# Attention and two gated layers on one core: the fp16 copy of P made by GpSimd, and attention steps dealt to slices by a table

## The chip, the cores and the metric

One core of a Trainium2 chip runs the whole program. The time is device microseconds of one execution; of several executions the median is given. TensorE (PE in the profile, its weight loads PEld) multiplies, VectorE (DVE) and ScalarE (ACT) work element by element, GpSimd (POOL) does selects, clearings and reductions across partitions, and SyncE (SP) issues nearly all DMAs, one after the other in its own order.

## The reference

Inputs are q, k, v of shape (4, 8, 576, 64), a memory `M_prev` and `z_prev` for each head, a gate `beta`, and the weights of two gated feed-forward layers. The reference computes:

```python
scores = where(causal, -1e9, scale * q @ k.T)     # 4 batches, 8 heads, 576 tokens
a      = softmax(scores);  local = a @ v
q_p    = phi(q);           mem   = (q_p @ M_prev) / (q_p @ z_prev + 1e-6)
x      = sigmoid(beta) * mem + (1 - sigmoid(beta)) * local       # 2304 tokens of 512
xn     = x / sqrt(mean(x*x) + 1e-6) * rms_g
x      = (silu(xn @ w_gate) * (xn @ w_val)) @ w_out               # d_ff 1536
out    = (sigmoid(x @ w_gate2) * (x @ w_val2)) @ w_out2
```

All inputs are fp32, and the kernel keeps nearly fp32 accuracy by splitting each operand of a product in a high and a low part (fp32r or fp16) and adding three products. The exponentials P of attention are such an operand.

## The kernel before, in words

The tokens are worked on in five groups. Group -1 holds the first 128 tokens of all four batches (512 tokens), groups 0 to 3 the other 448 tokens of one batch each. A group goes through both gated layers (l = 0 and 1), each cut into 12 slices of 128 hidden columns (f = 0 to 11), so 24 slices in a group. For each slice TensorE makes the gate and value products (`hidden`, 12 matmuls each, line 961), ScalarE and VectorE form the gated value and split it in two (`gated`, lines 981 to 1006), and TensorE adds the slice's share to the output (`out_share`, 12 matmuls, line 1027), one slice behind. The weights come from DRAM through SyncE's queue; in group -1 they are unpacked from 64-bit words, in group 0 they are turned into fp16 pairs (`halve`, lines 830 to 841: sums by ScalarE, an all-reduce by GpSimd at line 832, two scaled passes by ScalarE, two by VectorE) and written back, later they are loaded as pairs (line 903). In group 1 the output weights get the same treatment (`share_steps`, lines 752 to 778).

While the 24 slices of group g run, the attention of group g + 1 is made beside them. It is a list of steps (`att_steps`, 41 of them, 36 for the last), head by head: `v` loads V, `qk` loads and splits keys and queries (tiles kd and qd, one buffer each, lines 210 to 230), `sc` makes scores and the weights P, `av` multiplies P with V, `mem` adds the memory's part for two heads, `meas` measures q and k of the group after it, `vmax`, `vsplit`, `norm`, four `xT` and `units` do what their names say. The scores of a head are laid key by query, 1472 useful columns in a tile `sc`; ScalarE copies them from PSUM (line 550), GpSimd masks four blocks (line 555), VectorE takes the maximum over the key tiles (569, 572), GpSimd over the partitions (574), VectorE subtracts it (575, 580). Then `softmax_weights` (line 234) works in place: ScalarE makes the exponential (237), GpSimd clears the unused first columns of the two halves of P (241 or 244), ScalarE casts the exponential to fp16, the high half (246), and VectorE subtracts that from it, the low half (247). `att_av` uses both as weights (lines 589 to 591). For odd heads of groups 1 to 3 the halves lie in two spare tiles named top, otherwise in a tile pt.

The main loop decides after which slice a step is traced. `done` counts the output shares traced so far in the group (1 to 24). Before the change the share of the list was a straight line between two numbers of the group, kept in `HOLD` and `DUE`:

```python
total = 2 * NF - DUE[g + 1]
wait = HOLD[g + 1]
while used < len(steps) and used < len(steps) * (done - wait) // (total - wait):
    with behind(lagged(AFTER[g + 1])):
        steps[used]()
```

A step's instructions are put behind those of an earlier slice on ScalarE and VectorE (`lagged`), and the loads of a slice's weights behind those of another (`BACK`). Within these bounds the framework lays out each engine's order when the program is built, from the order in which instructions were traced and a model of their durations; on the chip each engine then keeps its order.

Of the kernel before, what the change touches and what calls it, by code (L numbers as in the profile page):

```python
# [10 lines left out]
F32R = mybir.dt.float32r  # L11
# [5 lines left out]
ALU = mybir.AluOpType  # L17
# [9 lines left out]
SW = 1536  # L27
# [8 lines left out]
NSHARE = (2, 1)  # L36

ONE = (1, 12)
DUE = (3, 6, 6, 5, 8)
HOLD = (1, 2, 1, 1, 1)  # L40
BACK = (3, 3)
AFTER = (3, 1, 3, 3)

# [25 lines left out]
def attn_moe_moe_kernel(ctx, tc, qT, kT, qk0, v, mz, beta, w8, rms_g, outT):  # L69
# [6 lines left out]
    nc = tc.nc  # L76
    B, H, D, S = qT.shape
# [3 lines left out]
    NF = w8.shape[1]  # L81
# [3 lines left out]
    const = ctx.enter_context(tc.tile_pool(name="const", bufs=1))  # L85
# [15 lines left out]
        out=tri, in_=tri, compare_op=ALU.is_ge, fill=NEG, base=0, pattern=[[1, 128]], channel_multiplier=-1  # L101
# [25 lines left out]

    q2_ring = []
    for i in range(2):
        t = const.tile([128, S], F32R, name=f"q2_{i}")  # L130
        nc.vector.memset(t[64:128].bitcast(F32), 0.0)
        q2_ring.append(t)
    vh1 = const.tile([128, 5, H, 65], F16, name="vh1")
# [71 lines left out]
    def att_qk(g, u):  # L205
        kd = ap_.tile([128, S], F32, tag="kd", bufs=1, name="kd")
        qd = ap_.tile([128, S], F32, tag="qd", bufs=1, name="qd")[:, 128:S]
        for src, dst, c0 in ((kT, kd, 0), (qT, qd, 128)):
            for j in range(2):
                nc.sync.dma_start(out=dst[64 * j:64 * j + 64], in_=src[g, u, :, c0:S])  # L210
        if g < HALVED:
            q2 = q2_ring[qring[0] % 2]
            qring[0] += 1
            kk = ap_.tile([128, S], F32R, tag="kk", bufs=2, name="kk")
            qq = ap_.tile([128, S], F32R, tag="qq", bufs=2, name="qq")[:, 128:S]
            q2 = q2[:, 128:S]
            nc.scalar.activation(out=kk, in_=kd, func=AF.Copy)
            nc.scalar.activation(out=qq, in_=qd, func=AF.Copy)
            for out, d, hi, r in ((kk, kd, kk, slice(64, 128)), (q2, qd, qq, slice(0, 64))):
                nc.vector.tensor_tensor(out=out[r], in0=d[r], in1=hi[r].bitcast(F32), op=ALU.subtract)  # L220
        else:
            kk = ap_.tile([128, 2, S], F16, tag="kk", bufs=2, name="kk")[:, 0]
            both = ap_.tile([128, 2, S], F16, tag="qq", bufs=2, name="qq")
            qq, q2 = both[:, 0, 128:S], both[:, 1, 128:S]
            nc.gpsimd.memset(q2[64:128], 0.0)
            qs = st["qs", g]
            nc.scalar.activation(out=kk, in_=kd, func=AF.Copy, scale=qs[:, 0:1])
            nc.scalar.activation(out=qq, in_=qd, func=AF.Copy, scale=qs[:, 1:2])
            for out, d, hi, i, r in ((kk, kd, kk, 0, slice(64, 128)), (q2, qd, qq, 1, slice(0, 64))):
                nc.vector.scalar_tensor_tensor(  # L230
                    out=out[r], in0=d[r], scalar=qs[r, i:i + 1], in1=hi[r], op0=ALU.mult, op1=ALU.subtract
                )
        st["qk", g, u] = kk, qq, q2

    def softmax_weights(sc, both, spare):
        sc = sc[:, 64:SW]
        nc.scalar.activation(out=sc, in_=sc, func=AF.Exp, scale=both)  # L237
        if spare:
            pt = [t.bitcast(F16) for t in tops]
            for t in pt:  # L240
                nc.gpsimd.memset(t[:, 0:64], 0.0)
        else:
            pt = ap_.tile([128, 2, SW], F16, tag="pt", name="pt")
            nc.gpsimd.memset(pt[:, :, 0:64], 0.0)
            pt = [pt[:, i] for i in range(2)]
        nc.scalar.copy(out=pt[0][:, 64:SW], in_=sc)
        nc.vector.tensor_tensor(out=pt[1][:, 64:SW], in0=sc, in1=pt[0][:, 64:SW], op=ALU.subtract)
        return pt

# [601 lines left out]
    for i in range(2):  # L851
        t = const.tile([128, SW // 2], I32, name=f"top{i}")
# [502 lines left out]
    def last_of(e):  # L1355
        return next(i for i in reversed(nc.cur_bb.bb.instructions) if i.engine == e)
# [80 lines left out]
    for g in range(-1, B):  # L1437
        n = 512 if g < 0 else S - 128
        steps = list(att_steps(g + 1)) if g + 1 < B else []
# [6 lines left out]
                shares[ONE[1] + f] += share_steps(0, f)  # L1446
            shares[ONE[1] + NF].append(lambda: share_units(0))

        total = 2 * NF - DUE[g + 1]

        wait = HOLD[g + 1]
        if g == 0:
            ring["w"] = NEARLY + NLATE
        done, used = 0, 0
        for l in range(2):
            early = 2 if g < 0 and l == 0 else 0
            ws, hs, halfway = early_ws[:early], early_hs[:early], []
            for f in range(early):
                hidden(ws[f], l, f, 256, g, xt, hs[f], 256, (("mm", "mm"), ("ps", "pa"))[f])
                halfway.append(tuple(last_of(e) for e in (mybir.EngineType.Activation, mybir.EngineType.DVE)))  # L1460
            po = None
            if g == B - 1:
                po = [late[f"po{d // 2}"].tile([128, NMAX], F32, tag=f"po{d}", name="po") for d in range(KD)]
                halves = xt if l == 0 else xh
                xs = token_sums(halves, "c" if l == 0 else "a")
                last_slices(l, n, xt, halves, xs, po)
            for f in range(0 if g == B - 1 else NF + 1):
                if f < NF:
                    if f >= early:
                        if g > 0 and l == 1 and f == NWIDE:  # L1470
                            unit_slices(g)
                        turn = lagged(BACK[g + 1]) if g <= 0 else []
                        if g < 0 and l == 1 and f in (2,):
                            turn = turn + evacuated
                        if g >= 0 and l == 0 and f in (1, 2):
                            turn = turn + tokens_done
                        with behind(turn + (halfway[-1:] if early and f < early + 3 else [])):
                            ws.append(weights(g, l, f))
                        hs.append(htiles(g, l, f))
                        if g == B - 2 and l == 1 and f == NF - 3:  # L1480
                            first_sums(0)
                        hidden(ws[f], l, f, n, g, xh if l == 1 and is_half(g, l, f) else xt, hs[f])
                        marks.append(tuple(last_of(e) for e in (mybir.EngineType.Activation, mybir.EngineType.DVE)))
                if f > 0:
                    if po is None:
                        po = [late[f"po{d // 2}"].tile([128, NMAX], F32, tag=f"po{d}", name="po") for d in range(KD)]
                    out_share(ws[f - 1], hs[f - 1], po, n, f == 1, f == NF)
                    done += 1
                    with ExitStack() as after:

                        if g < 0 and done < 5:
                            traced = nc.cur_bb.bb.instructions
                            for e in (mybir.EngineType.Activation, mybir.EngineType.DVE, mybir.EngineType.SP):
                                after.enter_context(
                                    tc.issue_after(next(i for i in reversed(traced) if i.engine == e))
                                )
                        for step in shares[done]:
                            with behind(lagged(2)):
                                step()
                        while used < len(steps) and used < len(steps) * (done - wait) // (total - wait):  # L1500
                            with behind(lagged(AFTER[g + 1])):
                                steps[used]()
                            used += 1
                            if used == len(steps):
                                tokens_done = [tuple(last_of(e) for e in (mybir.EngineType.Activation, mybir.EngineType.DVE))]
            if g < 0 and l == 0:
                begin.close()
            xn = wide_tokens("cd") if l == 0 else None
            for d in range(KD):
                evacuate(l, d, n, g, po[d], xn)  # L1510
            evacuated = [tuple(last_of(e) for e in (mybir.EngineType.Activation, mybir.EngineType.DVE))]
            if l == 0 and g >= 0:
                xh = half_tokens("b")
                with tc.high_priority(400):
                    halve_tokens(g, n, po, xh)
                    if g >= NSHARE[1]:
                        group_unit()
            if l == 0 and g < 0:
                with tc.issue_after(z["gm"]):
                    token_scale()  # L1520
            xt = xn
# [56 lines left out]
```

## Time and profile before

| what | value |
|---|---|
| median of 3 runs | 1013.51 us (1010.52 to 1014.92) |
| the profiled execution, its own time | 1016.42 us |
| its span, first to last instruction | 1014.6 us |
| mean granted TensorE clock | 0.996 |
| HBM read, written | 187.43 MB, 51.38 MB |

The span is from the first to the last instruction. The page gives the busy time of each engine; a busy TensorE need not be at its peak, since its matmuls overlap in the records. The chain is the work that ended last, followed back from the end to what released each piece. A line with an idle time says how long the engine stood before it and what ended that. DMA issues of SyncE stand on its timeline as SPq.

### The profile page before, as it was taken

What the parts mean: (1) busy time and instruction counts of PE and PEld (TensorE: products, weight loads), DVE (VectorE), ACT (ScalarE), POOL (GpSimd) and SP (SyncE); (2) the same over time, 40 slices, a digit from 0 to 9 for tenths busy, and PEclk for the clock granted to TensorE, in tenths of its full rate; (3) what the DMA queues carried; (4) which work ended last, traced back from release to release, by engine and by line L of the source; (5) the groups of instructions that cost most, each with busy time, mean ns of one, the idle gap of its engine ahead of it and who ended that gap; (6) DMA issues with size and microseconds to landing.
All of it is one profiled execution on the core that took longest, in us unless ns stands there. A gap on an engine that the chain in (4) does not pass through costs nothing.

```text
span 1014.6 us, 19021 instructions
## 1 busy us (share of the span) xinstructions
PE 999.3 (98%) x6721; PEld 700.0 (69%) x6721; DVE 832.1 (82%) x1826; ACT 654.7 (65%) x1238; POOL 201.8 (20%) x339
## 2 busy tenths in 40 slices
PE   9999999999999999999999999999999999999998
PEld 6878887888666676666666765555567556876885
DVE  6989999997769998775998977757779776995883
ACT  7668887786678888674778676535456353543452
POOL 4203221141004233300424432002133100000000
PEclk9999999999999999999999999999999999999999
DMA  9599998986894676498779856995544256836521
GB/s 350 180 373 398 345 352 257 376 308 200 272 368 172 224 251 229 177 322 240 246 257 322 266 179 224 309 340 167 174 144 167 83 159 212 284 135 226 201 84 37
DMA packets 102561, 243.74 MB, mean 240 GB/s; under 512 B 25154, under 2 KB 37058, under 8 KB 102466
## 3 DMA queue, kind: packets, MB, share of 16 engines
q1 hardware_dynamic: 102322, 242.41, 69.8%
q8 instruction: 53, 0.87, 0.3%
q14 instruction: 42, 0.34, 0.1%
q10 hardware_dynamic: 144, 0.11, 0.0%
HBM read 187.43 MB, written 51.38 MB: 235 GB/s over the span
## 4 chain that ended last, share of the span: by engine, by line
PE 65%; DVE 14%; issue 9%; DMA 6%; ACT 5%; POOL 1%; SPq 0%; DVEq 0%; POOLq 0%; ACTq 0%
PE po L1027 20%; PE pg L961 16%; PE pv L961 15%; PE pw L1137 7%; PE ps L253 2%; DMA qd<-in_qT 1%; PE pm L638 1%; POOL sc L555 1%; DVE mx L572 1%; DMA raw<-in_w 1%; DMA wr<-kept 1%; PE pav L589 1%; PE pav L591 1%; PE pav L590 1%; DVE w L878 1%
## 5 line engine op out<-in xcount | busy, mean ns | idle before, releaser
L555 POOL TENSOR_SCALAR_AFFINE_SELECT sc<-sc 128x128 f32<-128x128 f32 (+1 forms) x128 | 73.0, 583 | 194.1 <-ACT sc L550 193.3
L1027 PE MATMUL po<-h,ws 128*128 128x448 f16 (+2 forms) x468 | 107.6, 375 | 0.0
L961 PEld LDWEIGHTS <-ws 128*128 128x128 f16 x552 | 53.5, 99 | 53.1 <-issue 4.9
L1027 PE MATMUL po<-h,wl 128*128 128x448 f16 (+2 forms) x372 | 86.8, 376 | 0.1
L961 PEld LDWEIGHTS <-wr 128*128 128x128 f16 x552 | 52.8, 98 | 49.2 <-issue 3.5
L1027 PE MATMUL po<-h,wr 128*128 128x448 f16 (+1 forms) x384 | 84.9, 364 | 0.2 <-ACT h L1005 0.2
L574 POOL PARTITION_ALL_REDUCE mb<-mx x32 | 61.3, 1915 | 70.9 <-DVE mx L572 62.1
L981 ACT ACTIVATE t<-pg,unit 128x448 f32<-128x448 f32 x70 | 43.8, 626 | 40.3 <-PE pg L961 40.1
L550 ACT COPY sc<-ps 128x512 f32<-128x512 f32 (+1 forms) x96 | 52.7, 562 | 18.6 <-PE ps L253 18.5
L1027 PEld LDWEIGHTS po<-h,ws 128*128 128x128 f32 x300 | 55.9, 188 | 9.4
L961 PEld LDWEIGHTS <-wl 128*128 128x128 f16 x360 | 34.7, 98 | 31.7 <-issue 1.3
L253 PE MATMUL ps<-qq,kk 128*128 128x64 f16 (+2 forms) x280 | 53.2, 295 | 0.0
L237 ACT ACTIVATE sc<-sc,qs 128x1472 f32<-128x1472 f32 x24 | 36.6, 1526 | 23.4 <-DVE sc L580 15.4
L990 DVE SCALAR_TENSOR_TENSOR t<-t,pv 128x448 f32<-128x448 f32 (+1 forms) x52 | 32.7, 629 | 18.6 <-PE pv L961 18.3
L1027 PEld LDWEIGHTS po<-h,wl 128*128 128x128 f32 x228 | 42.5, 188 | 8.0 <-ACT h L998 0.5
L1027 PE MATMUL po<-h,wrl 128*128 128x448 f16 (+1 forms) x192 | 44.0, 374 | 1.6 <-ACT h L1005 1.4
L983 DVE SCALAR_TENSOR_TENSOR t<-t,pg 128x448 f32<-128x448 f32 (+2 forms) x50 | 30.9, 618 | 15.4 <-ACT t L981 15.3
L872 ACT ACTIVATE top<-raw 128x512 f16<-128x512 bf16 x50 | 38.0, 784 | 5.6 <-DMA raw<-in_w 4.4
L998 ACT CAST h<-t 128x448 fp32r<-128x448 f32 (+1 forms) x46 | 27.0, 586 | 19.6 <-DVE t L986 14.4
L572 DVE TENSOR_TENSOR mx<-mx,sc 128x320 f32<-128x320 f32 (+2 forms) x96 | 34.5, 359 | 4.0 <-POOL sc L555 3.1
L1155 ACT COPY sn<-pw 128x224 f32<-128x224 f32 x54 | 18.2, 341 | 30.0 <-PE pw L1137 27.9
L878 DVE SCALAR_TENSOR_TENSOR w<-raw,top 128x512 int32<-128x512 int32 x48 | 35.3, 747 | 0.8 <-ACT top L872 0.6
(437 smaller groups left out, 2870.0 us busy)
## 6 DMA issues: line engine op xcount, KB each, us to landing
raw<-in_w SPq DMA_DIRECT2D x50, 511.8 KB, 6.4
kept<-w SPq DMA_DIRECT2D x48, 256.0 KB, 5.2
ws<-parts SPq DMA_DIRECT2D x24, 512.0 KB, 5.4
wr<-half SPq DMA_DIRECT2D x23, 512.0 KB, 4.1
rawl<-in_w SPq DMA_DIRECT2D x22, 511.8 KB, 6.5
wr<-parts SPq DMA_DIRECT2D x21, 512.0 KB, 5.6
ws<-half SPq DMA_DIRECT2D x21, 512.0 KB, 4.7
kd<-in_kT SPq DMA_DIRECT2D x64, 144.0 KB, 3.5
```

The costliest lines, as they stand in the source:

```text
L237: nc.scalar.activation(out=sc, in_=sc, func=AF.Exp, scale=both)
L253: nc.tensor.matmul(ps[:, c0:c0 + n], kk[:, k0:k0 + 128], r[:, q0 - 128:q0 - 128 + n], start=(i == 0), stop=(i == 1))
L550: nc.scalar.copy(out=sc[:, o:o + c], in_=ps[:, 0:c])
L555: nc.gpsimd.affine_select(out=d, in_=d, compare_op=ALU.is_ge, fill=NEG, base=SQ[kt] - T0[kt], pattern=[[1, n]], channel_multiplier=-1,)
L572: nc.vector.tensor_tensor(out=mx[:, q:448], in0=mx[:, q:448], in1=sc[:, d:d + 448 - q], op=ALU.max)
L574: nc.gpsimd.partition_all_reduce(mb[:, 0:448], mx[:, 0:448], channels=128, reduce_op=bass_isa.ReduceOp.max)
L872: nc.scalar.activation(out=top.bitcast(F16).rearrange("p (n t) -> p n t", t=2)[:, :, 1], in_=raw.bitcast(BF16)[:, :, 2], func=AF.Copy)
L878: nc.vector.scalar_tensor_tensor(out=dst.bitcast(I32), in0=raw.rearrange("p n t -> p (n t)").bitcast(I32).rearrange("p (n t) -> p n t", t= ...
L961: nc.tensor.matmul(ps[:, 0:n], w[:, a, k * 128:(k + 1) * 128], x[b][:, k, o:o + n], start=(i == 0), stop=(i == 3 * KD - 1))
L981: nc.scalar.activation(out=t, in_=pg[:, 0:n], func=AF.Tanh, scale=u[:, 0:1] if half else 0.5)
L1027: nc.tensor.matmul(po[d][:, 0:n], w[2][:, a, c], hh[:, b, 0:n], start=(first and i == 0), stop=(last and i == 2))
L1137: nc.tensor.matmul(regions[m][at], left(i, m, a, k), right(j, b, k), start=first and c == 0, stop=c == 5, skip_group_check=True,)
```

## The change

The cast of the exponentials to fp16 leaves ScalarE. GpSimd makes it with a select whose condition always holds (the pattern is constant, base 1 is never below 0), reading fp32 and writing fp16. VectorE's subtract then waits for GpSimd in place of ScalarE.

```diff
-        nc.scalar.copy(out=pt[0][:, 64:SW], in_=sc)
+        nc.gpsimd.affine_select(
+            out=pt[0][:, 64:SW], in_=sc, compare_op=ALU.is_ge, fill=0.0, base=1, pattern=[[0, SW - 64]],
+            channel_multiplier=0,
+        )
         nc.vector.tensor_tensor(out=pt[1][:, 64:SW], in0=sc, in1=pt[0][:, 64:SW], op=ALU.subtract)
```

The straight line gives way to a table with an entry for each step: the count of shares after which it is traced. The first row is for group -1, the last for group 2.

```diff
-DUE = (3, 6, 6, 5, 8)
-HOLD = (1, 2, 1, 1, 1)
+DEAL = (
+    (2, 2, 3, 3, 4, 4, 5, 5, 6, 6, 7, 7, 8, 8, 9, 9, 10, 10, 11, 11, 12, 12, 13, 13, 14, 14, 15, 15, 16, 16, 17, 17, 18, 18, 19, 19, 20, 20, 21, 21, 21),
+    (3, 3, 4, 4, 4, 5, 5, 6, 6, 6, 7, 7, 8, 8, 8, 9, 9, 10, 10, 10, 11, 11, 11, 12, 12, 15, 15, 15, 15, 15, 15, 15, 15, 15, 16, 17, 17, 17, 18, 20, 20),
+    (2, 2, 3, 3, 4, 4, 4, 4, 4, 4, 4, 5, 5, 6, 6, 6, 6, 6, 6, 6, 6, 7, 9, 11, 12, 12, 13, 13, 14, 14, 14, 15, 17, 18, 18, 18, 19, 19, 20, 20, 20),
+    (2, 2, 3, 3, 4, 4, 5, 5, 6, 6, 7, 7, 8, 8, 9, 9, 10, 10, 11, 11, 12, 12, 13, 13, 14, 14, 15, 15, 16, 16, 17, 17, 18, 18, 19, 19),
+)
...
-                        while used < len(steps) and used < len(steps) * (done - wait) // (total - wait):
+                        while used < len(steps) and DEAL[g + 1][used] <= done:
```

Written out as steps, the rows for groups 0 and 1 against the old formula, from the slice where they part:

```
group 0   old                        new
  13      sc6 qk7 av5                -
  14      mem2 meas2                 -
  15      sc7 av6 av7                sc6 qk7 av5 mem2 meas2 sc7 av6 av7 mem3
  16      mem3 meas3                 meas3
  17      norm xT0 xT1               norm xT0 xT1
  18      xT2 xT3 units              xT2
  20      -                          xT3 units
group 1   old                        new
   4      qk1 sc1 vsplit             qk1 sc1 vsplit qk2 av0 sc2 qk3
   5      qk2 av0                    av1 mem0
   6      sc2 qk3 av1                meas0 sc3 qk4 av2 sc4 qk5 av3 mem1
   7      mem0 meas0                 meas1
   8      sc3 qk4                    -
   9      av2 sc4 qk5                sc5
  10      av3 mem1                   -
  11      meas1 sc5 qk6              qk6
 12-14    (av4 sc6, qk7 av5, mem2 meas2 sc7 in both)
  15      av6 av7                    av6
  16      mem3 meas3 norm            -
  17      xT0 xT1                    av7
  18      xT2 xT3 units              mem3 meas3 norm
  19      -                          xT0 xT1
  20      -                          xT2 xT3 units
```

Last, the low halves' tile of the queries in group -1's attention is allocated with the 448 columns that are used.

```diff
-        t = const.tile([128, S], F32R, name=f"q2_{i}")
+        t = const.tile([128, S - 128], F32R, name=f"q2_{i}")
...
-            q2 = q2[:, 128:S]
```

## Rows read from the trace of the kernel before

**Rows 1.** the page, parts 1 and 4: busy us, then the chain

```profile
PE 999.3 (98%) x6721; PEld 700.0 (69%) x6721; DVE 832.1 (82%) x1826; ACT 654.7 (65%) x1238; POOL 201.8 (20%) x339
PE 65%; DVE 14%; issue 9%; DMA 6%; ACT 5%; POOL 1%; SPq 0%; DVEq 0%; POOLq 0%; ACTq 0%
```

**Rows 2.** groups 0, 1: busy us of PE, PEld, DVE, ACT, POOL

```profile
265.00:476.00 211.00, 207.74 (x1367) 139.26 (x1366) 169.73 (x397) 156.05 (x329) 46.02 (x92) 0.99 0.76 257
476.00:674.00 198.00, 195.02 (x1320) 123.98 (x1318) 164.80 (x418) 136.38 (x248) 56.67 (x93) 0.99 0.78 266
```

**Rows 3.** the chain, group 0: start us, us, what

```profile
446.44 2.27 PE pv L961 x12
448.71 2.44 PE po L1027 x12
```

**Rows 4.** a stretch: us, PE busy, granted clock, DMA, GB/s

```profile
583.50:587.50 4.00, 4.00 (x13) 0.57 0.35 117
```

**Rows 5.** all waits, waiter <- releaser: us, times, longest

```profile
PE pg L961 <- DVE t L983: 1.6, 3, 0.7
PE pav L591 <- DVE pt L247: 0.2, 1, 0.2
DVE t L983 <- ACT t L981: 15.5, 10, 3.6
POOL sc L555 <- ACT sc L550: 193.3, 69, 21.8
```

**Rows 6.** timeline, stall A: start, us, what [idle before <-releaser]

```profile
425.53 0.67 PE L1027 MATMUL po<-h,wrl 128*128 128x448 f32 x2 [1.37 <-ACT h L1005]
426.48 3.71 PE L1027 MATMUL po<-h,wrl 128*128 128x448 f32 x10 [0.28 <-DVE h L1006]
420.01 0.36 POOL L832 PARTITION_ALL_REDUCE wtop<-sums  x1 [4.05 <-ACT ws L830]
421.57 0.74 POOL L555 TENSOR_SCALAR_AFFINE_SELECT sc<-sc 128x128 f32<-128x128 f32 x1 [1.19 <-ACT sc L550]
```

**Rows 7.** timeline, stall B: VectorE, SyncE, TensorE

```profile
574.03 0.82 DVE L230 SCALAR_TENSOR_TENSOR kk<-kd,qs,kk 64x576 f16<-64x576 f32 x1
574.88 1.11 SPq L210 DMA_DIRECT2D kd<-in_kT  x2
578.47 0.58 SPq L903 DMA_DIRECT2D ws<-half  x1
583.43 4.13 PE L961 MATMUL pg<-hb,ws 128*128 128x448 f16 x12 [1.84 <-DMA ws<-half]
```

**Rows 8.** line 246: ns min/median/max; who waited: us, times

```profile
L246 ACT CAST pt<-sc x20: 1392/1407/1459, 102.7 to 791.3; 128x1472 f16<-128x1472 f32 x20
L246 ACT CAST top<-sc x12: 1401/1418/1421, 333.4 to 812.8; 128x1472 f16<-128x1472 f32 x12
  DVE top L247: 3.8, 5
  DVE pt L247: 1.5, 3
```

**Rows 9.** GpSimd: busy us, mean ns; last row ns min/median/max

```profile
L100 POOL TENSOR_SCALAR_AFFINE_SELECT tri<-tri 128x128 f32<-128x128 f32 x1 | 0.3, 292 | 0.0
L555 POOL TENSOR_SCALAR_AFFINE_SELECT sc<-sc 128x128 f32<-128x128 f32 x96 | 55.2, 591 | 84.5 <-ACT sc L550 84.3
L422 POOL TENSOR_SCALAR e<-e 128x512 f32<-128x512 f32 x4 | 6.0, 1496 | 7.4 <-ACT e L418 7.4
L555 POOL TENSOR_SCALAR_AFFINE_SELECT sc<-sc x128: 238/364/3715, 73.6 to 802.3; 128x128 f32<-128x128 f32 x96, 128x64 f32<-128x64 f32 x32
```

**Rows 10.** timeline, ScalarE and VectorE, one head in group 1

```profile
565.69 1.52 ACT L237 ACTIVATE sc<-sc,qs 128x1472 f32<-128x1472 f32 x1
568.83 1.46 ACT L246 CAST pt<-sc 128x1472 f16<-128x1472 f32 x1
571.52 1.78 DVE L247 TENSOR_TENSOR pt<-sc,pt 128x1472 f16<-128x1472 f32 x1
```

More of the change, by code (lines that the diff above doesn't have):

```diff
@@ L1447, in attn_moe_moe_kernel @@
             shares[ONE[1] + NF].append(lambda: share_units(0))
-        total = 2 * NF - DUE[g + 1]
-        wait = HOLD[g + 1]
         if g == 0:
```

## The prediction

> **What bounds the kernel now.** I read the page's shares first. TensorE is busy 999.3 us of a span of 1014.6 us, VectorE 832.1, ScalarE 654.7, GpSimd 201.8; on the chain of work that ended last TensorE holds 65%, VectorE 14% and ScalarE 5%, about 51 us, with everything that it does [rows 1]. So ScalarE's cast can be worth only what it makes others wait.
>
> Next the table by stage. In groups 0 and 1 (during each of them the attention of the group after it runs beside the slices) VectorE is busy 169.73 of 211 us and 164.80 of 198 us, 80 and 83% [rows 2]: it is the engine nearest to TensorE, and attention gives it its load.
>
> A busy TensorE is not one at its peak, so I look at its pace. Undisturbed, twelve matmuls of 448 columns take 2.27 us, and the twelve of an output share with fp32r hidden values 2.44 us [rows 3]. The change touches no matmul. All that can be won is time in which TensorE stands or runs below that pace. Two places make up most of it.
>
> Stall A, in group 0. TensorE waits 1.37 us and then 0.28 us for the hidden values, and the next ten matmuls take 3.71 us, where ten of the twelve in 2.44 us would take 2.03 [rows 3, 6]: 1.37 + 0.28 + 1.68 = 3.3 us. GpSimd shows why: the all-reduce of a weight's sums (L832) waited 4.05 us for ScalarE, and a head's mask select, behind it in GpSimd's order, came at 421.57 only [rows 6]. VectorE's maxima wait for the masks, and the slice's own product stands behind them.
>
> Stall B, in group 1. The load of half-precision weights (ws from half) is issued at 578.47; TensorE waits 1.84 us for it, and its next twelve matmuls take 4.13 us in place of 2.27 [rows 3, 7]; the granted clock just there is 0.57, the lower level of 1.2 GHz, after the engine had stood [rows 4]. That is 1.84 + 1.86 = 3.7 us. SyncE's order shows why: the loads of the next keys (kd) were let go at 574.88, as VectorE had just made the last head's low halves (L230, 574.03 + 0.82), and the weights' load stood behind them [rows 7].
>
> **The change part by part.**
> *ScalarE loses the cast*, 20 times 1.407 and 12 times 1.418 us, 45.2 us in all [rows 8]. VectorE's subtract waited for it in 8 of 32 heads, 3.8 + 1.5 us together [rows 8]. So most of the 45.2 us is taken from where nobody waits, beside TensorE's matmuls. What it can give is an earlier tanh: VectorE waited 15.5 us in ten places for ScalarE's tanh (L981), TensorE 1.6 us in three places for the VectorE instruction behind it (L983), and 0.2 us for a subtract [rows 5]. I count these last two, 1.8 us, as gone.
>
> *GpSimd gains 32 selects of 128x1472, fp32 in, fp16 out.* No such instruction is in the trace. From below: the select at the start took 292 ns for 128 columns, and the fastest mask of all 238, which I take for one of 64 columns [rows 9]; that is 0.84 ns for a further column, and 0.292 + 1344 x 0.00084 = 1.4 us, as much as the cast. From above: the masks of 128 columns average 591 ns [rows 9], and 1472/128 of that is 6.8 us. Between them lies GpSimd's other pass over one fp32 tensor, 512 columns in 1496 ns [rows 9], which makes 4.3 us. I take 1.4 us stretched as the masks are on average, by 591/292 = 2.0: 2.9 us. 93 us more on an engine that is busy 201.8 is no bound.
>
> The masks' spread, up to 3715 ns for at most 128 columns, says that something holds GpSimd while it runs [rows 9]. The Trainium skill (GPSIMD Engine Reference, Specifications) says that GpSimd shares its SBUF interfaces with VectorE and contends with VectorE instructions that have two SBUF inputs. The masks' spread agrees with that rule.
>
> *A head's own chain* is exp, copy, subtract, product with V. In one head of group 1 the exp ended at 567.21, the cast ran from 568.83 to 570.29 and the subtract began at 571.52 [rows 10]: a select of 2.9 us, begun at once, ends at 570.1, a little earlier. Where the cast followed the exp at once, the select is 2.9 - 1.4 = 1.5 us later. That can be so in the 8 heads whose subtract waited; TensorE felt one of them [rows 5, 8]. I count one, 1.5 us lost.
>
> *GpSimd's order.* Before, GpSimd cleared the first columns of P and went on. Now it stands at the select until the exp is done, and behind it stand the next head's masks, the clearing of q2 and the all-reduces of the weights' sums. GpSimd stood 193.3 us waiting for copies of scores alone [rows 5], so there is room, but in order only. I put nothing in the sum; the price is in the second rival.
>
> *The table.* By the old formula, the first and last row of DEAL are the old slices one by one: groups -1 and 2 get the select and nothing else. In group 1 (third row) heads 0 to 4 come forward, seven and eight steps in slices 4 and 6, head 5's scores at 9 in place of 11; slices 12 to 14, around the change of layers, keep the steps that they had, and the end moves from 18 to 20. So VectorE comes to head 6's low halves without the backlog, kd is let go earlier, and the weights behind it too: SyncE needs to be let go some 2 us earlier. I count stall B, 3.7 us, as gone. In group 0 (second row) slices 13 and 14 get nothing and nine steps stand in slice 15. That clears VectorE at the change of layers, but puts two heads beside the halving of weights, where stall A was: I count half of it, 1.7 us. Each step that moves takes its loads along in SyncE's order: in group 0 kd and qd of head 7 (13 to 15), the loads for attention's memory part and the next group's measuring; in group 1 those of heads 2 to 5, forward. The later ends in both groups (slice 20) are covered: attention's tokens are due at the next group's start, after slice 24. If that cover went, each slice of delay would cost up to some 8 us (211 us over 24 slices and the change of layers) [rows 2]; four slices are left.
>
> *q2's tile is cut to the columns that are used*: a smaller clearing on VectorE at the start, beside the first loads, nothing.
>
> **The sum.** -3.7 - 1.7 - 1.8 + 1.5 = -5.7 us on the profiled execution's 1016.42 us (its span and 1.8 us around it): 1010.7. That execution was 2.9 us above the median of the runs shown, 1013.51. On the median the forecast is 1007.8 us.
>
> **The rivals.**
> *The stalls only move.* For it: stall A came from nothing but the order on GpSimd; that order is made anew everywhere, nine steps stand in one slice, and GpSimd stands at every exp. Against: stall B's queue is visibly relieved. If A and B are replaced by their like, -1.8 + 1.5 is left: about 1013.
> *The select is slow and the head late.* By the 512-column pass it takes 4.3 us, by the masks' mean 6.8. It decides from some 4.3 us on, the time from the end of exp to the subtract in the head above [rows 10]. The 8 heads whose subtract waited then hand TensorE at least 4.3 - 2.9 = 1.4 us each: 1007.8 + 11 = 1019, slower; at 6.8 us it would be 8 x 3.9 = 31 us, 1039. For it: VectorE's load [rows 2] and the mask of 3715 ns [rows 9]. Against: once VectorE itself stands at the subtract, it no longer disturbs the select. The rule of the Trainium skill on the shared interfaces speaks for this rival.
> *More goes than I count*: stall A wholly, and as much as that again in places too small to list, 1.7 + 3.3 = 5 us: 1003.
> *GpSimd doesn't make the copy in one pass*, or the table is not followed: nothing in the diff speaks for it, and I give it nothing.
>
> **How the numbers follow.** Forecast 0.45, stalls move 0.24, slow select 0.15, more 0.16. 0.5%, about what a measurement of this kernel can tell from no change, is 5 us: faster is below 1008.4, slower above 1018.6. Of the forecast's 0.45, 0.28 lie below 1008.4; with the 0.16, faster is 0.44. Same is 0.17 + 0.24 = 0.41, slower 0.15. The range leaves out the slow rival and the far end of the gain: 1000 to 1017. The forecast's own range is 1004 to 1011.
>
> **What would show it.** Right: 32 selects of 2 to 4 us in L246's place; ws from half gone from TensorE's waits and the granted clock at its upper level where layer 2 of group 1 starts; VectorE's wait at the subtract below some 15 us in all. Wrong: selects above 4.3 us, products with V that wait for the subtract in several heads, or masks and all-reduces that start just behind a select while VectorE and then TensorE wait for them. Group 2 tells the two parts apart: its row of the table is unchanged, so what changes there is the select's.

## The result: slower, 1026.92 us

| | before | after |
|---|---|---|
| median | 1012.08 us (1010.52 to 1014.92) | 1026.92 us (1025.5 to 1028.11) |
| profiled execution | 1016.42 us | 1028.11 us |

The ratio is 1.0143, 95% interval 1.0126 to 1.016: 14.8 us more, where 5.7 us less was forecast. The time lies above the range.

The page's shares and the chain of the kernel after, beside [rows 1]:

```profile
PE 1000.1 (97%) x6721; PEld 698.4 (68%) x6721; DVE 851.6 (83%) x1826; ACT 614.9 (60%) x1206; POOL 256.1 (25%) x371
PE 56%; DVE 14%; issue 12%; DMA 10%; ACT 5%; POOL 2%; SPq 1%; POOLq 0%; DVEq 0%; ACTq 0%
```

ScalarE lost 39.8 us and GpSimd gained 54.3, as the change intends. TensorE is busy as before. But VectorE, for which the diff changes only a clearing at the start, is busy 19.5 us more, with the same 1826 instructions. Windows over groups 0 and 1, to be held against [rows 2] (start and end of the window, its length, busy time and instructions of PE, PEld, DVE, ACT, POOL, granted clock, DMA share, GB/s):

```profile
267.70:481.50 213.80, 205.90 (x1362) 137.71 (x1361) 172.21 (x392) 143.93 (x317) 62.41 (x99) 1.00 0.74 251
481.50:685.00 203.50, 196.92 (x1327) 124.24 (x1326) 176.40 (x422) 129.37 (x244) 63.60 (x102) 0.99 0.77 257
```

VectorE has 814 instructions in the two (815 before) and takes 348.61 us for them in place of 334.53. In group 1 it is busy 11.6 us more and the group lasts 5.5 us longer.

The selects themselves are quicker than forecast, 1.68 and 1.50 us:

```profile
L249 POOL TENSOR_SCALAR_AFFINE_SELECT pt<-sc 128x1472 f16<-128x1472 f32 x20 | 33.6, 1678 | 44.4 <-ACT sc L240 44.3
L249 POOL TENSOR_SCALAR_AFFINE_SELECT top<-sc 128x1472 f16<-128x1472 f32 x12 | 18.0, 1503 | 30.2 <-ACT sc L240 30.2
```

What beside them took longer is seen in VectorE's groups of instructions. First before: a product of one column (L766), the low halves of the weights (L696), the first maximum over the scores (L569).

```profile
L696 DVE TENSOR_TENSOR ws<-w,ws 128x512 fp32r<-128x512 f32 x36 | 24.8, 689 | 0.9 <-ACT ws L695 0.9
L569 DVE TENSOR_TENSOR mx<-sc 128x448 f32<-128x448 f32 x32 | 20.1, 630 | 2.8 <-POOL sc L555 2.5
L766 DVE TENSOR_TENSOR shared<-inv,unit 128x1 f32<-128x1 f32 x10 | 1.5, 148 | 0.0
```

The same three groups after (L772, L702, L575):

```profile
L702 DVE TENSOR_TENSOR ws<-w,ws 128x512 fp32r<-128x512 f32 x36 | 26.8, 746 | 1.2 <-ACT ws L701 1.2
L575 DVE TENSOR_TENSOR mx<-sc 128x448 f32<-128x448 f32 x32 | 22.5, 703 | 2.4 <-POOL sc L561 2.2
L772 DVE TENSOR_TENSOR shared<-inv,unit 128x1 f32<-128x1 f32 x10 | 3.9, 392 | 0.0
```

A product of one column can't become 2.6 times as long by its work. One of them, in the timeline of after, at a select:

```profile
563.01 1.71 POOL L249 TENSOR_SCALAR_AFFINE_SELECT top<-sc 128x1472 f16<-128x1472 f32 x1 [0.69 <-ACT sc L240]
563.45 1.29 DVE L772 TENSOR_TENSOR shared<-inv,unit 128x1 f32<-128x1 f32 x1
```

It is recorded from 563.45 to 564.74, and the select ends at 564.72: the product stood until then, and the profile books its standing as VectorE's busy time. How that reaches TensorE is seen right behind it. VectorE went from one instruction to the next without a pause, and the product with the gate (L989), whose turn came after three others, began at 565.78; TensorE, done with a share, stood 1.35 us for it:

```profile
565.78 0.61 DVE L989 SCALAR_TENSOR_TENSOR t<-t,pg 128x448 f32<-128x448 f32 x1
566.44 2.05 PE L967 MATMUL pg<-ha,wl 128*128 128x448 f16 x10 [1.35 <-DVE t L989]
```

The tanh that this product needs had ended at 563.47, so up to 1.14 us of the 1.35, the time that the small product stood, are the select's. In the whole trace of after, twenty VectorE instructions that began while a select ran are more than 0.15 us longer than the median of their kind before, by 17.2 us together.

TensorE's waits after, beside [rows 5] (what it waited for: us in total, times, longest), and three of VectorE's (at the tanh, and at the subtract):

```profile
PE pg L967 <- DVE t L989: 4.0, 4, 2.0
PE po L1033 <- ACT h L1004: 2.1, 3, 1.3
PE pg L967 <- DMA ha<-x: 2.0, 2, 1.5
PE pv L967 <- DVE t L992: 1.8, 2, 0.9
PE pg L967 <- DMA ws<-half: 0.4, 1, 0.4
...
DVE t L989 <- ACT t L987: 19.3, 12, 5.9
...
DVE top L253 <- POOL top L249: 7.0, 4, 5.1
DVE pt L253 <- POOL pt L249: 5.0, 4, 1.3
```

### The profile page after: what moved, and what is told of

It is laid out like the page before. It is cut to its first block, busy times and chain, and to the rows that moved or that the text cites. A ratio compares the mean times of both kernels' runs of the same rounds, so it can differ in the third digit from the quotient of the medians.

```text
span 1026.3 us, 19057 instructions
## 1 busy us (share of the span) xinstructions
PE 1000.1 (97%) x6721; PEld 698.4 (68%) x6721; DVE 851.6 (83%) x1826; ACT 614.9 (60%) x1206; POOL 256.1 (25%) x371
## 4 chain that ended last, share of the span: by engine, by line
PE 56%; DVE 14%; issue 12%; DMA 10%; ACT 5%; POOL 2%; SPq 1%; POOLq 0%; DVEq 0%; ACTq 0%
PE po L1033 16%; PE pg L967 14%; PE pv L967 13%; PE pw L1143 7%; PE ps L259 2%; DMA ph<-in_qT 1%; POOL sc L561 1%; DMA out_T<-o 1%; DMA kept<-w 1%; DVE t L992 1%; DMA ws<-half 1%; DVE qq L233 1%; DMA out<-ws 1%; PE pav L595 1%; DVE t L989 1%
## 5 line engine op out<-in xcount | busy, mean ns | idle before, releaser
L1033 PE MATMUL po<-h,ws 128*128 128x448 f16 (+2 forms) x468 | 109.7, 377 | 0.3 <-ACT h L1004 0.3
L240 ACT ACTIVATE sc<-sc,qs 128x1472 f32<-128x1472 f32 x24 | 36.6, 1524 | 19.0 <-DVE sc L586 12.6
L989 DVE SCALAR_TENSOR_TENSOR t<-t,pg 128x448 f32<-128x448 f32 (+2 forms) x50 | 30.8, 616 | 19.2 <-ACT t L987 19.1
L249 POOL TENSOR_SCALAR_AFFINE_SELECT pt<-sc 128x1472 f16<-128x1472 f32 x20 | 33.6, 1678 | 44.4 <-ACT sc L240 44.3
L1011 ACT ACTIVATE h<-t,shared 128x448 f16<-128x448 f32 x30 | 19.9, 666 | 35.0 <-DVE t L996 34.9
L765 POOL PARTITION_ALL_REDUCE otop<-osum x22 | 14.8, 673 | 95.3 <-ACT wl L763 44.4
```

The costliest lines, as they stand in the source:

```text
L249: nc.gpsimd.affine_select(out=pt[0][:, 64:SW], in_=sc, compare_op=ALU.is_ge, fill=0.0, base=1, pattern=[[0, SW - 64]], channel_multiplier=0,)
L989: nc.vector.scalar_tensor_tensor(out=t, in0=t, scalar=1.0, in1=pg[:, 0:n], op0=ALU.add, op1=ALU.mult)
L1033: nc.tensor.matmul(po[d][:, 0:n], w[2][:, a, c], hh[:, b, 0:n], start=(first and i == 0), stop=(last and i == 2))
```

## The experiments

Theory, from these rows: while a select runs on GpSimd, a VectorE instruction with two SBUF inputs stands (called the hold below); VectorE pays, then TensorE. Rivals: the table of slices; GpSimd's standing at each exp, which delays what is behind it; the longer way from exp to product.

Below, "old slices" means DEAL rows that give the slices of the old formula. The ratios are to the kernel before.

| kernel | median us | ratio, 95% interval | VectorE busy | ScalarE | GpSimd |
|---|---|---|---|---|---|
| before (profile) | | | 832.1 | 654.7 | 201.8 |
| after | 1026.92 | 1.0143 (1.0126 to 1.016) | 851.6 | 614.9 | 256.1 |
| e1 select, old slices | 1025.27 | 1.0116 (1.0084 to 1.0148) | 852.7 | 614.0 | 259.1 |
| e2 cast, new table | 1014.11 | 1.0013 (0.9996 to 1.0031) | 831.4 | 653.3 | 199.4 |
| e3 cast, group 0's new row | 1015.94 | 1.0008 (0.9988 to 1.0029) | 831.1 | 654.8 | 200.7 |
| e4 cast, group 1's new row | 1013.70 | 1.0005 (0.999 to 1.002) | 833.5 | 653.4 | 201.9 |
| e5 select of 16 columns | 1012.16 | 0.9996 (0.998 to 1.0012) | 832.0 | 654.3 | 212.6 |
| e6 cast, unread selects beside it | 1023.03 | 1.0100 (1.0079 to 1.0121) | 847.7 | 653.7 | 294.1 |
| e7 select in four | 1031.38 | 1.0186 (1.0171 to 1.0201) | 845.7 | 615.0 | 284.5 |
| e8 select of half the columns | 1018.88 | 1.0051 (1.0033 to 1.0069) | 837.4 | 636.2 | 226.3 |
| e9 cast, unread memsets beside it | 1014.17 | 1.0005 (0.9995 to 1.0015) | 834.3 | 655.6 | 261.5 |
| e10 two masks in one | 1016.06 | 1.0025 (1.0012 to 1.0038) | 833.3 | 654.6 | 189.2 |

And by stage, from the profiled executions: how much later than in before the first matmul of a group's last output share but one began, in us. (The last share itself is mixed with the first products of the next group, not in the same order in every kernel.) Before's own execution lay 3 to 4 us above before's medians of 1012.08 to 1013.51. By the columns e2, e3, e5 and e9, all about 4 us ahead at the end of group 0, it lost them in that group, so that -4 from there on is no gain.

| end of group | after | e1 | e8 | e6 | e7 | e5 | e9 | e2 | e3 | e4 |
|---|---|---|---|---|---|---|---|---|---|---|
| -1 | +3.2 | +2.1 | +0.7 | +2.0 | +3.3 | -0.3 | -0.9 | -0.2 | -0.2 | -0.4 |
| 0 | +5.3 | +3.8 | -2.1 | -0.5 | +11.0 | -4.5 | -3.9 | -4.1 | -4.0 | -1.8 |
| 1 | +11.0 | +8.7 | +1.1 | +6.2 | +14.6 | -4.4 | -0.8 | -3.8 | -0.6 | -4.5 |
| 3 | +11.7 | +8.4 | +1.8 | +6.9 | +15.4 | -4.6 | -1.2 | -2.2 | -0.5 | -2.8 |

**The two parts alone.** e1 keeps the select with the old slices; e2 keeps the new table with ScalarE's cast; e3 and e4 take one new row each.

```
e2, against after:
-        nc.gpsimd.affine_select(
-            out=pt[0][:, 64:SW], in_=sc, compare_op=ALU.is_ge, fill=0.0, base=1, pattern=[[0, SW - 64]],
-            channel_multiplier=0,
-        )
+        nc.scalar.copy(out=pt[0][:, 64:SW], in_=sc)
```

> The select stays with GpSimd, the table holds the old formula's slices in all four rows. Theory 1 (the select itself costs: while it runs, VectorE's instructions with two inputs from SBUF stand, and GpSimd stands at each exp): group -1 and group 2, whose rows the change left alone, lost 3.2 and 0.9 us, so four groups lose some 6 to 10 us and this comes at 1018 to 1022 us, with VectorE about 14 us busier than before. Theory 2 (the table's bursts cost, the select nothing): 1012 to 1016, the 3.2 us of group -1 staying and the losses of groups 0 and 1 gone. Theory 3 (any change lays the engines' orders anew, and that alone moves stalls by several us either way): anything from 1005 to 1022, with stalls in places of their own.

> The cast stays with ScalarE, the new table is followed. Theory 1: the table is not what costs, 1008 to 1014 us, with stall B of group 1 gone. Theory 2: the bursts in slice 4 and 6 of group 1 and slice 15 of group 0 hold TensorE just as in the changed kernel, 1019 to 1025. Theory 3: no tie between the two, stalls in other places again.

> The cast stays with ScalarE, and of the new table only the row of group 0 is followed. Theory 2: the loss between the start of group 0 and the start of group 1 (3.6 us in the changed kernel) is there, groups 1 and 2 are as before: about 1016. Theory 1: about 1010 to 1012, stall A (3.3 us) gone or halved.

> The cast stays with ScalarE, and of the new table only the row of group 1 is followed. Theory 2: V's split and two heads' loads and splits fall into slice 4 together, VectorE comes late to a slice's product there as in the changed kernel (2.0 us and then the slow matmuls), about 1016. Theory 1: stall B (3.7 us) is gone, about 1008 to 1010.

The select alone makes the kernel 1.16% slower, which is more than I expected (1018 to 1022 us, VectorE 14 us busier); the table alone changes nothing that can be told, so the gains that I gave e3 and e4 didn't come, nor, clear of the noise, the losses of the other theory. VectorE's 20 us come with the select and go with it. After and e1 overlap, so what the table costs beside a select stays open. Group 2, by which the prediction meant to tell the two parts apart, added only 0.8 us in after; group -1, whose row is an old one too, added 3.2.

**GpSimd's order.** In e5 GpSimd stands at every exp as in after, but copies only 16 columns; ScalarE casts the other 1456. Old slices.

```
         nc.gpsimd.affine_select(
-            out=pt[0][:, 64:SW], in_=sc, compare_op=ALU.is_ge, fill=0.0, base=1, pattern=[[0, SW - 64]],
+            out=pt[0][:, 64:80], in_=sc[:, 0:16], compare_op=ALU.is_ge, fill=0.0, base=1, pattern=[[0, 16]],
...
+        nc.scalar.copy(out=pt[0][:, 80:SW], in_=sc[:, 16:])
```

> Old table; GpSimd's select makes 16 of the 1472 columns and ScalarE casts the other 1456. GpSimd still stands in its order until the exp is done, VectorE's subtract still waits for it, but it runs for 0.2 us. Theory 1a (the running select holds VectorE): as before, 1011 to 1016. Theory 1b (GpSimd's standing at the exp, with masks and all-reduces behind it): as with the select alone, 1022 to 1027. Theory 3 (new order, new stalls): between.

As before, 0.9996 (0.998 to 1.0012): the order costs nothing that can be told.

**The select without the relief.** e6 keeps cast and old slices and adds, on GpSimd, three selects of the same columns into a tile that nobody reads.

```
e6, against before:
...
+        for c, n in ((0, 512), (512, 512), (1024, 448)):
+            nc.gpsimd.affine_select(
+                out=junk[:, 0:n], in_=sc[:, c:c + n], compare_op=ALU.is_ge, fill=0.0, base=1, pattern=[[0, n]],
+                channel_multiplier=0,
+            )
```

> Old table; ScalarE casts as before, and GpSimd makes three selects of 512, 512 and 448 columns of the exponentials into a scratch tile that nobody reads. VectorE's subtract waits for ScalarE alone. Theory 1a: VectorE is held nearly as with the select (a little less, since it can go on between the three), 1018 to 1025, with VectorE some 10 to 15 us busier. Theory 1b: 1022 to 1027. If the cost lies in the subtract waiting for GpSimd, or in ScalarE's new order: 1011 to 1015.

Nothing waits for the copy that these selects make, and the time rises by 1%, so the longer way from exp to product isn't needed for the loss. VectorE's busy time rises by 15.6 us:

```profile
PE 998.4 (98%) x6721; PEld 698.0 (68%) x6721; DVE 847.7 (83%) x1826; ACT 653.7 (64%) x1238; POOL 294.1 (29%) x435
```

**The bench.** Nothing but GpSimd passes over 1472 columns and, beside them, six VectorE instructions of 448 columns of each kind.

> Not the reference's computation: only a bench that writes zeros to the output. Six VectorE instructions of one kind beside no GpSimd work, and beside rows of GpSimd passes over 1472 columns (select to fp16, select to fp32, memset, tensor_scalar, cast). Theory 1 says that a running select holds VectorE's instructions with two SBUF inputs until it ends, so that the first of the six takes its own 0.6 us or up to 1.4 us more, that those with one SBUF input and PSUM run as alone, and that whichever of the two engines came second waits. A rival (GpSimd alone gives way, as I read the masks before) has all VectorE durations as without GpSimd, and the selects stretched.

VectorE's groups alone, in the stretch from 7 to 23 us: two SBUF inputs (L65), one of two inputs in PSUM (L71), one fp32 SBUF input (L74).

```profile
L65 DVE TENSOR_TENSOR z<-x,y 128x448 f32<-128x448 f32 x6 | 3.7, 624 | 0.2
L71 DVE SCALAR_TENSOR_TENSOR z<-x,ps 128x448 f32<-128x448 f32 x6 | 3.7, 619 | 0.2
L74 DVE TENSOR_SCALAR z<-x 128x448 f32<-128x448 f32 x6 | 2.4, 392 | 0.2
```

Beside selects of fp32 to fp16, from 27 to 75 us:

```profile
L45 POOL TENSOR_SCALAR_AFFINE_SELECT sel<-a 128x1472 f16<-128x1472 f32 x30 | 45.2, 1507 | 1.8
L65 DVE TENSOR_TENSOR z<-x,y 128x448 f32<-128x448 f32 x6 | 10.4, 1731 | 0.2
L74 DVE TENSOR_SCALAR z<-x 128x448 f32<-128x448 f32 x6 | 9.0, 1497 | 0.2
L71 DVE SCALAR_TENSOR_TENSOR z<-x,ps 128x448 f32<-128x448 f32 x6 | 3.7, 618 | 0.2
L77 DVE TENSOR_REDUCE z<-x 128x1 f32<-128x448 f32 x6 | 3.7, 618 | 0.2
```

Beside memsets, from 124 to 163 us:

```profile
L56 POOL MEMSET sel<- 128x1472 f32 x28 | 37.7, 1347 | 1.4
L74 DVE TENSOR_SCALAR z<-x 128x448 f32<-128x448 f32 x6 | 8.9, 1476 | 0.2
L65 DVE TENSOR_TENSOR z<-x,y 128x448 f32<-128x448 f32 x6 | 3.7, 624 | 0.2
```

An instruction with two SBUF inputs takes 1731 ns beside selects, 624 alone, and that holds for all six, not only for the first as I expected; with one of its inputs in PSUM it takes the same 618. So GpSimd isn't alone in giving way. Beside memsets, which read nothing, it isn't held. A pass over one fp32 input is held by both, 1497 and 1476 ns in place of 392. The Trainium skill (SBUF — State Buffer, section "SBUF: two separate sides") says that the ports which VectorE and GpSimd share are an exclusive lock, that the instruction which starts first has them to its end, and that a VectorE instruction with two SBUF inputs needs them only against a GpSimd one that reads SBUF. The bench and the row at 563.45 agree.

**Length and kind.** If the hold is the price, half a select costs less, and memsets of like length cost nothing. e8 selects 736 columns and casts 736 on ScalarE. e9 keeps the cast; GpSimd takes one column of the exp, so that it stands there, and clears a tile that nobody reads. Old slices in both.

```
e8, against after:
+            out=pt[0][:, 64:800], in_=sc[:, 0:736], compare_op=ALU.is_ge, fill=0.0, base=1, pattern=[[0, 736]],
...
+        nc.scalar.copy(out=pt[0][:, 800:SW], in_=sc[:, 736:])
e9, against before:
         nc.scalar.copy(out=pt[0][:, 64:SW], in_=sc)
...
+        nc.gpsimd.tensor_copy(junk[:, 0:1], sc[:, 0:1])
+        for n in (512, 512, 448):
+            nc.gpsimd.memset(junk[:, 0:n], 0.0)
```

> The slices of the kernel before; GpSimd's select copies the first 736 columns of a head, ScalarE's cast the other 736. Theory (a VectorE instruction with two SBUF inputs stands until the select beside it has ended): selects of some 0.75 us hold VectorE about half as long as those of 1.41-1.68 us did, so VectorE is busy 840 to 845 us (832 without a select, 852.7 with the whole one) and the time is 1016 to 1021. Rival (it is the head's order, GpSimd standing at the exp and two engines to wait for, and not the length of the select): 1023 to 1026 as with the whole select, or 1012 as with the select of 16 columns.

> The kernel before and its slices, ScalarE's cast kept. GpSimd also copies one column of each head's exp and then clears 512, 512 and 448 columns of a tile that nobody reads, where the kernel that came to 1023.03 made three selects of these widths. In the bench a memset didn't hold VectorE's instructions with two SBUF inputs (625 ns) but held those of fp32 with one SBUF input (394 to 1474 ns). Theory (the hold is the price): VectorE busy 832 to 838 us and 1011 to 1016. Rival (GpSimd is busy then, and what stands behind it in its order is late): 1020 to 1025, with VectorE's busy time unchanged.

e8 comes to 1.0051, between the two ends, as the theory had it; the 5.3 us that VectorE is busier are under the 8 to 13 expected. The selects of 736 columns took 1056 and 910 ns. e9 decides between the hold and a GpSimd that is merely busy and late. Its GpSimd is busier than after's and stands at the exp as well, and the time is 1.0005:

```profile
PE 996.4 (98%) x6721; PEld 698.9 (69%) x6721; DVE 834.3 (82%) x1826; ACT 655.6 (65%) x1238; POOL 261.5 (26%) x467
```

Its memsets, in GpSimd's groups:

```profile
L253 POOL MEMSET junk<- 128x512 f16 (+1 forms) x96 | 49.5, 515 | 4.5
```

They last 49.5 us. e6's selects last 90.0, but after's 51.6, and after is 1.4% slower. Counted as in after, VectorE's instructions beside the added GpSimd work are 1.0 us longer in e9 (five of them), 5.9 in e8 and 15.1 in e6.

**Two ways to do better, both misses.** e7 cuts the select into four of 368 columns (old slices), so that a held instruction gets in between. e10 leaves the cast and makes one select of 128x2x128 of the masks of key tiles 2 and 3.

```
e7, against after:
+        for c in range(0, SW - 64, 368):
+            nc.gpsimd.affine_select(
+                out=pt[0][:, 64 + c:432 + c], in_=sc[:, c:c + 368], compare_op=ALU.is_ge, fill=0.0, base=1,
+                pattern=[[0, 368]], channel_multiplier=0,
+            )
e10, against before:
+                    if kt == 2:
+                        d = sc[:, 896:SW].rearrange("p (k q) -> p k q", k=2)[:, :, 128:256]
...
+                        pattern=[[0, 2], [1, n]] if kt == 2 else [[1, n]],
```

> Old table; GpSimd makes the copy in four selects of 368 columns. Theory 1a: VectorE slips in between, a held instruction waits 0.4 us at most in place of 1.4, VectorE's extra busy time falls from 15 us to 5 or 10, and the time to 1016 to 1021. Theory 1b: no better than with one select, 1024 to 1028, since GpSimd stands at the exp all the same and works a little longer.

> The kernel before and its slices, cast on ScalarE; of the four mask selects of a head the last two (key tiles 2 and 3) become one select of 128x2x128, so 96 in place of 128. A version that could beat both. Theory (VectorE pays for the time that GpSimd's passes last beside it): only the fixed part of 32 selects goes, some 0.2 us each of 0.29, about 6 us of GpSimd's time, of which VectorE feels a part: 1008 to 1013. Rival (the merged mask must wait for the later of two score copies and VectorE's maxima come later): 1012 to 1016.

e7 is the slowest of all, against what I expected. VectorE is 13.6 us busier, less than in e1, but the selects cut in four last 80.2 us in all (687 and 618 ns each), the whole ones 51.6. The largest part of its loss is in group 0, where TensorE waits for attention's tokens (ha<-x) and for a product with the gate, up to 4.1 and 3.2 us:

```profile
PE pg L968 <- DMA ha<-x: 4.6, 2, 4.1
PE pg L968 <- DVE t L990: 3.5, 2, 3.2
```

Longer heads and later tokens fit that; no run takes one of them away, so the cause isn't settled. e10 has 12.6 us less on GpSimd, and is 0.25% slower. The maxima waited longer for the masks (7.0 us, by the two rows before 5.6), as its rival said.

## Why the prediction was wrong

**The step that failed** is the one on GpSimd's gain, which ended "93 us more on an engine that is busy 201.8 is no bound", and its reading of the masks' spread: "something holds GpSimd while it runs". The contention was seen and priced in one direction, as a stretch of the select. It is mutual: the select took 1.68 and 1.50 us in place of the 2.9 that I took, and VectorE, of which the prediction itself said that it is nearest to TensorE, paid 19.5 us. The sum has no term for that. The time rose by 0.6 to 1.0 us for each us of VectorE's in four kernels (after 14.8 for 19.5, e1 12.1 for 20.6, e6 10.5 for 15.6, e8 5.4 for 5.3); in e7 it rose by 18.8 for 13.6, which the hold alone doesn't explain. A hint stood in the trace of before: one line of VectorE's with two SBUF inputs, in two shapes, min, median and max:

```profile
L999 DVE TENSOR_TENSOR h<-t,h x46: 609/678/1265, 61.6 to 562.0; 128x448 fp32r<-128x448 f32 x24, 128x512 fp32r<-128x512 f32 x22
```

Its two longest, 1265 and 1016 ns, have 448 columns, and no other of that shape takes more than 630. Both stood beside an all-reduce on GpSimd, the longer one here:

```profile
523.05 2.04 POOL L574 PARTITION_ALL_REDUCE mb<-mx  x1 [0.73 <-DVE mx L572]
523.63 1.26 DVE L999 TENSOR_TENSOR h<-t,h 128x448 fp32r<-128x448 f32 x1
```

I looked for long instructions on GpSimd [rows 9] and not on VectorE.

**ScalarE's relief shows no gain.** The short waits, 1.8 us, were to go with an earlier tanh. VectorE waited 19.3 us in twelve places for the tanh (15.5 in ten before, [rows 5]), TensorE 4.0 for the product behind it (1.6). ScalarE has 40 us less, and the tanh is not earlier where it counts. No run has the relief without a select, so its own worth stays open.

**Stall B** went as the prediction said: ws from half costs 0.39 us, and the eight matmuls behind it take 1.69 us, in the timeline of after:

```profile
596.13 1.69 PE L967 MATMUL pg<-hb,ws 128*128 128x448 f16 x8 [0.39 <-DMA ws<-half]
```

The window around it has the granted clock at 1.00:

```profile
594.00:600.00 6.00, 5.62 (x29) 3.88 (x27) 6.00 (x16) 5.97 (x14) 3.45 (x5) 1.00 0.76 270
```

e4, which has only that row of the table, has no stall B, gains 2.7 us in group 1 (-1.8 to -4.5 in the table by stage) and loses 1.7 of it again by the end. e2, with the whole table, has none either, but waits 2.01 us for other weights at 494.73 and gains nothing in group 1. In both, TensorE then waits 1.27 us at the start of group 2 for ScalarE's copy of an output, a wait that no kernel with group 1's old slices shows. And e8 lost stall B with the old slices. So the term held for the one place and not for the group: that the stalls only move was the prediction's own rival. In after a like stall stands earlier in the group. VectorE waited 3.65 us there for an output tile that was still being written (1.04 in before); behind that its gate product came 9.55 us later than in before (487.02 against 477.47), TensorE's shares only 7.9. The slack between the two was gone, and TensorE stood at 505.17, in the timeline:

```profile
483.51 0.63 DVE L1257 TENSOR_SCALAR o<-po 128x448 f32<-128x448 f32 x1 [3.65 <-DMA out_T<-o]
...
505.17 4.12 PE L967 MATMUL pg<-ha,ws 128*128 128x448 f16 x12 [1.96 <-DVE t L989]
```

After it had stood, the granted clock was 0.58, the lower level of 1.2 GHz, as the window shows:

```profile
505.00:509.00 4.00, 3.83 (x12) 1.65 (x12) 3.94 (x8) 3.08 (x7) 2.37 (x3) 0.58 0.51 171
```

By [rows 3] that costs 1.96 + 4.12 - 2.27 = 3.8 us, the price of stall B. (Both are some 0.2 us too high: a timeline row of twelve such matmuls at full pace is 2.43 us long, and 2.27 is the chain's.) e1, with the old slices, has a wait of 2.0 us in the same place, so it isn't the new row's.

**Stall A** was, as far as these runs can tell, not there to be won. e5 and e9, with before's own slices, end group 0 about 4 us ahead of before's profile, and their medians are before's: that profile seems to have a loss that most executions don't have, though no second trace of before shows it. My 1.7 us were worked out from one execution and then taken off the median. The reason was misread too: the mask at 421.57 stood behind the all-reduce in GpSimd's order, but GpSimd had idled 1.19 us before it for ScalarE's copy of the scores [rows 6], so the all-reduce didn't make it late.

**The table's cover** may have a hole. "Attention's tokens are due at the next group's start" was right, and at the start of group 1 TensorE waits for them: 1.47 us in after, 2.10 in e3, 1.01 in e2, not at all in before. From the mark at the end of group 0 to the first share of group 1, e3 loses 3.9 us and e2 1.2. But e8 and e9 lose 1.7 and 1.8 there with the old slices, so how much of it is the new row's stays open. As a whole the table, for which I counted 5.4 us, is worth nothing that can be told: 1.0013 (0.9996 to 1.0031).

**A head's chain and GpSimd's order** were about right, the select's own time aside. VectorE waited 12.0 us at the subtract (7.0 + 5.0; 5.3 before), under the 15 that I set as the limit; TensorE's waits down to 0.4 us hold none for the subtract. The order costs nothing that can be told (e5). The rival that ended slower, 1019 and above, had the sign for another reason: its select was to take over 4.3 us.

## What to carry over

Work given to GpSimd beside a loaded VectorE is to be priced on both engines: list VectorE's instructions with two SBUF inputs, and its fp32 passes over one, in the stages concerned, and take the added pass as time in which they may stand. Look for that first in the trace at hand, in the longest ones of VectorE's shortest forms; the held time is booked as busy, so no wait of the held engine shows it. And ask first who on the path waits for the engine that is relieved: of the 40 us off ScalarE no gain is to be seen here.

## What the runs showed of the hardware

A GpSimd pass that reads SBUF held VectorE instructions with two SBUF inputs for as long as it ran: beside a min with a constant on GpSimd (3.92 us for 1472 columns) single ones of 625 ns took 3451 to 3581. On GpSimd the copy of 1472 columns to fp16 took 1.41 us at the least, as a cast and as a select alike. Not held were an instruction with one of two inputs in PSUM and a maximum over one SBUF input (618 ns each); held by memsets too was an fp32 pass over one SBUF input, 1476 ns in place of 392.
